# Chunk 4's first MLP layer by twenty block products, with chunk 5's substitution running on into chunk 4's second layer

## The chip, the cores and the metric

The kernel runs on one core of one Trainium2 chip. The time is that of the device in microseconds (us), from launch to end of one execution. TensorE is called PE, VectorE DVE, ScalarE ACT, GpSimd POOL, and SP is the engine whose queue issues nearly all DMAs. Instructions stand in a fixed order on each engine and the engines wait for each other by semaphores.

## The reference, cut to what matters

A DeltaNet layer (4 batches, 8 heads, 768 tokens, head size 48) is followed by an MLP of 3072 tokens, 384 inputs and 2048 hidden values, all in float32:

```python
for t in range(S):                      # per batch and head
    y[t]   = q[t] @ state
    v_old  = state.T @ k_n[t]           # k_n: k over its length
    state += beta[t] * outer(k_n[t], v[t] - v_old)
x = y.transpose(0, 2, 1, 3).reshape(B * S, H * D)
h = x @ w_in
g = h * (1.0 / (1.0 + np.exp(-h)))      # silu
out = g @ w_out
```

## The kernel before

The 768 tokens are cut into six chunks (0 to 5) of 128 tokens, each of two halves of 64. Within a chunk the recurrence is a triangular system; its 32 by 32 diagonal blocks are inverted and then merged to 64 by 64. For each chunk these stages run:

- `prepare`: scores of keys and queries, `ap`, and the blocks, which are laid out anew through DRAM to stand one system per partition (`blocks`, `g`).
- `invert` (L683 on): the substitution, on DVE alone. For m from 31 down to 1 two instructions each (L688 forms `rank`, L693 adds it to `x`), 62 in all, with 31 to 256 elements per partition. Then `g` (L706) and `x` (L697) are scaled. `g` is written to DRAM as `low` and read back as `xe` (L717), `x` as `up` and read back as `xi` and the rest of `xe`, all by SP's queue.
- `solve`: two merges on PE (`merge`, L847: the first reads `xe` and `ap` into `py`, which is copied to `y`; the second reads `xi`, `xe` and `y` into `px`, which is copied to `xi`), then for each half the keys on the state (`ph`, L893), the inner values (`pz`), the update of the state (`pu`, and L932 on DVE), and the outputs, which end as `xT`, the MLP's inputs, by ACT's copies and five DMAs.
- the MLP's first layer, silu on ACT, and the second layer `combine` (L1451), in seven chains of eight products for each half, with sums of the hidden values on DVE between (`sum_g`, L1428) and the output's parts added into `o` (L1462) by way of one tile `kept`.

Both layers save products by forming sums of blocks. The first layer of chunks 2 to 4 is `hidden_by_products` (22 items per half of the hidden blocks, 44 in all, each of two matmuls of 128 by 128 with 256 columns). Chunk 5 alone uses `hidden_by_chains` (`BY_CHAINS`): products of sums of weights and sums of inputs, in chains that add up in one PSUM bank, each partial result read out after its item. There are 40 items of two matmuls. Items go round four banks, so an item's bank was last written four items before, and must have been read out by then: the first result for an output is copied by ACT (16 items), the others are added by DVE (24 items, `evacuate`). The sums of weights (`W_SUMS`, 16 and two that restore a quarter of `w_in`) overwrite parts of `w_in`, so they can only be made once no later chunk needs the old form; the sums of inputs (`X_SUMS`) number twelve.

The order is written out by hand. The solve of chunk c+1 is laid between the second layer's products of chunk c, and the substitution of chunk c+1 between the first layer's items of chunk c. `run(n)` issues n pieces of the MLP; a piece of the second layer is half a chain, four products. `paced` issues the substitution: each item of the layer earns it a credit, less where DVE has an addition to make, and it steps as long as the credit is positive. `run_to(start(c) + ITEMS + 3)` sets how many pieces lie between the first layer's end and the solve. Every instruction is pinned behind the one before it on its engine, so what DVE makes late is late for all that stands behind it there.

## Time and profile before

| | us |
|---|---|
| median of three runs | 626.05 |
| single runs | 623.24, 626.05, 772.2 |
| the profiled execution | 622.51 |
| its span, first to last instruction | 620.8 |
| PE busy | 606.4 (98%) |
| DVE busy | 466.6 (75%) |
| ACT busy | 247.7 (40%) |
| chunk 3's second layer, with chunk 4's solve | 403.4 to 458.3 |
| chunk 4's first layer, with chunk 5's substitution | 458.3 to 496.3 |
| chunk 4's second layer, with chunk 5's solve | 496.3 to 545.7 |
| chunk 5's first layer | 545.7 to 580.6 |

The profile is one execution as the hardware recorded it; times in it are from the span's start. A row of the timeline has the start, the duration, the engine, the line, what is written and read, and how many instructions were run together; in brackets stands how long the engine had been idle and what it waited for. The table by stages gives for each stretch its length, and for each engine the busy time and the number of instructions.

### The profile page before, as it was taken

The page shows a single profiled execution, that of the slowest core. Times are in us where ns is not written, and L with a number is a line of the kernel's source. Part 1 is how long each engine was busy: PE and PEld are TensorE (multiplying, and loading weights), DVE is VectorE, ACT ScalarE, POOL GpSimd, SP SyncE. Part 2 cuts the span into 40 slices and gives each one's busy share as a digit, 9 for nine tenths or more (in the row PEclk, how much of TensorE's full clock was granted, in tenths as well). Part 3 has the DMA queues.
Part 4 walks back from the last instruction along what each step waited for, and adds up shares of the span by engine and source line. Part 5 has one row for each costly group of instructions (what it writes and reads, how often), then busy time and mean ns, then how long its engine had stood idle before and what let it go on. Part 6 is the DMA issues. An engine that isn't in the chain of part 4 may idle for free.

```text
span 620.8 us, 21912 instructions
## 1 busy us (share of the span) xinstructions
PE 606.4 (98%) x9554; PEld 531.2 (86%) x9554; DVE 466.6 (75%) x983; ACT 247.7 (40%) x562; POOL 82.7 (13%) x83
## 2 busy tenths in 40 slices
PE   8889999999999999999999999999999999999997
PEld 5678778666689988888899998899998899988997
DVE  5856879998889976768986769976869997535632
ACT  3656756142351133533433533434433414445310
POOL 5443621247000010000010000010000020000000
PEclk9859999999999999999999999999999999999999
DMA  7745654164426482236073436084351060110011
GB/s 156 181 101 167 219 141 106 52 162 117 114 48 132 93 145 51 66 80 123 0 150 92 103 78 122 1 157 105 87 111 34 1 112 17 40 25 1 2 25 26
DMA packets 143935, 55.06 MB, mean 89 GB/s; under 512 B 113488, under 2 KB 137296, under 8 KB 143840
## 3 DMA queue, kind: packets, MB, share of 16 engines
q1 hardware_dynamic: 143360, 53.00, 37.9%
q8 instruction: 75, 1.23, 0.8%
q10 hardware_dynamic: 480, 0.67, 0.3%
q14 instruction: 20, 0.16, 0.1%
HBM read 40.99 MB, written 10.49 MB: 83 GB/s over the span
## 4 chain that ended last, share of the span: by engine, by line
PE 56%; DVE 1%; issue 0%; ACT 0%; DVEq 0%; ACTq 0%
PE px L1451 14%; PE py L1451 10%; PE hu L1168 10%; PE hx L1168 8%; PE hx L1335 3%; PE hu L1335 3%; PE pa L585 2%; PE pz L905 1%; PE ph L893 1%; PE pyc L986 1%; PE pyc L973 1%; PE pu L925 1%; PE px L847 1%; PE py L847 1%; DVE kq L1285 1%
## 5 line engine op out<-in xcount | busy, mean ns | idle before, releaser
L1114 PE MATMUL phid<-xT,w_in 128*128 128x256 f32 x384 | 89.1, 385 | 0.2 <-issue 0.2
L1114 PEld LDWEIGHTS phid<-xT,w_in 128*128 128x128 f32 x384 | 71.0, 190 | 10.4 <-issue 0.8
L1451 PE MATMUL px<-sums_of_w,sums_of_g 128*128 128x192 f32 x320 | 58.0, 330 | 0.0
L1451 PE MATMUL py<-w_out,sums_of_g 128*128 128x192 f32 x320 | 57.5, 329 | 0.0
L1451 PEld LDWEIGHTS px<-sums_of_w,sums_of_g 128*128 128x128 f32 x320 | 52.1, 190 | 1.1 <-issue 0.7
L688 DVE SCALAR_TENSOR_TENSOR rank<-g,step,x 128x31 f32<-128x31 f32 (+15 forms) x124 | 49.6, 400 | 4.6 <-DMA g<-blocks 1.7
L1451 PEld LDWEIGHTS py<-w_out,sums_of_g 128*128 128x128 f32 x320 | 52.3, 190 | 0.6
L693 DVE TENSOR_TENSOR x<-x,rank 128x31 f32<-128x31 f32 (+15 forms) x124 | 42.5, 342 | 4.4
L521 POOL TENSOR_TENSOR vf<-vf,n_slot 128x768 f32<-128x768 f32 x10 | 15.4, 1552 | 189.9 <-DVE sums_of_g L1428 147.2
L1428 DVE TENSOR_TENSOR sums_of_g<-gT 128x512 f32<-128x512 f32 (+2 forms) x44 | 28.0, 668 | 13.3 <-PE py L1451 13.1
L1462 DVE TENSOR_TENSOR o<-o,kept 128x192 f32<-128x192 f32 (+1 forms) x29 | 12.4, 426 | 32.6 <-ACT kept L1459 32.4
L1168 PE MATMUL hx<-xT,w_in 128*128 128x256 f32 x144 | 36.0, 379 | 0.0
L600 ACT COPY gT<-hu 128x512 f32<-128x512 f32 x36 | 21.1, 586 | 32.9 <-PE hu L1168 22.9
L1168 PE MATMUL hu<-xT,w_in 128*128 128x256 f32 x144 | 34.0, 379 | 0.0
L600 ACT COPY xT<-pyc 48x128 f32<-48x128 f32 (+2 forms) x120 | 31.1, 260 | 1.6
L932 DVE TENSOR_TENSOR state<-state,pu 48x384 f32<-48x384 f32 x44 | 24.3, 552 | 8.8 <-PE pu L925 7.8
L1168 PEld LDWEIGHTS hu<-xT,w_in 128*128 128x128 f32 x144 | 27.4, 190 | 3.7
L1168 PEld LDWEIGHTS hx<-xT,w_in 128*128 128x128 f32 x144 | 27.3, 190 | 3.6
L1451 PE MATMUL px<-sums_of_w,gT 128*128 128x192 f32 x160 | 28.7, 329 | 0.2 <-issue 0.2
L1451 PE MATMUL py<-w_out,gT 128*128 128x192 f32 x160 | 28.9, 330 | 0.0
L1451 PE MATMUL px<-w_out,gT 128*128 128x192 f32 x160 | 28.5, 329 | 0.0
L1122 ACT ACTIVATE gT<-phid 128x512 f32<-128x512 f32 x24 | 14.4, 598 | 35.5 <-PE phid L1114 35.3
(264 smaller groups left out, 1243.4 us busy)
## 6 DMA issues: line engine op xcount, KB each, us to landing
vf<-in_v_dram SPq DMA_DIRECT2D x48, 96.0 KB, 2.7
out_dram<-o SPq DMA_DIRECT2D x42, 96.0 KB, 2.3
w_out<-in_moe_w_in_dram SPq DMA_DIRECT2D x12, 256.0 KB, 3.4
sums_of_w<-in_moe_w_out_dram SPq DMA_DIRECT2D x8, 384.0 KB, 3.6
blocks<-ap SPq DMA_DIRECT2D x40, 64.0 KB, 2.3
g<-blocks SPq DMA_DIRECT2D x4, 512.0 KB, 3.5
up<-x SPq DMA_DIRECT2D x4, 512.0 KB, 3.0
xi<-up SPq DMA_DIRECT2D x16, 128.0 KB, 3.5
```

The costliest lines, as they stand in the source:

```text
L521: done = pin(nc.gpsimd.tensor_tensor(out=vf, in0=vf, in1=of, op=ALU.mult))
L585: pin(nc.tensor.matmul(pa[e][half, p * n * W : (p + 1) * n * W], lhsT=kq[rows, p, 0, half], rhs=kq[rows, p, js[0] : js[-1] + 1, half], sta ...
L600: return pin(nc.scalar.copy(to, of))
L688: pin(nc.vector.scalar_tensor_tensor(out=tv, in0=g[:, 0:m, m : m + 1].to_broadcast([P, m, n]), scalar=step[:, m : m + 1], in1=x[:, m : m + ...
L693: yield pin(nc.vector.tensor_tensor(out=x[:, 0:m, m:T], in0=x[:, 0:m, m:T], in1=tv, op=ALU.add))
L932: pin(nc.vector.tensor_tensor(out=to, in0=to, in1=by_heads(pu[of]), op=ALU.add))
L1114: pin(nc.tensor.matmul(ph[:, j * GT : (j + 1) * GT], lhsT=w_in[:, a, (2 * f + j) * P : (2 * f + j + 1) * P], rhs=xTs[c, hf][:, a, :], star ...
L1122: pin(nc.scalar.activation(out=hidden_of(c, hf, f), in_=ph[:], func=ACTF.Silu, scale=0.5))
L1168: pin(nc.tensor.matmul(to[:, GT * i : GT * (i + 1)], lhsT=weights[:, f], rhs=moving, start=start and i == 0, stop=True, skip_group_check=True,
L1335: pin(nc.tensor.matmul(to[:, GT * i : GT * (i + 1)], lhsT=weights[:, 2 * u + i], rhs=moving, start=start and i == 0, stop=True, skip_group ...
L1428: pin(nc.vector.tensor_tensor(out=sums_of_g[:, k, fs], in0=of[0], in1=of[1], op=op))
L1451: pin(nc.tensor.matmul(to, lhsT=at, rhs=quarter(f, *b) if isinstance(b, tuple) else sums_of_w[b][:, f], start=start and n == 0, stop=n == ...
```

## The change

`BY_CHAINS` takes in chunk 4 (`NCH - 2`), so both last chunks form their first layer by 40 items. What follows from that:

- The 18 sums of weights are made one chunk earlier, in three blocks of six in chunk 3's second layer; they are ordered anew, since two of their rooms lie in the key buffer that chunk 4's solve still reads.
- The twelve sums of inputs are made for both chunks, in three parts (six ahead of the layer, four at its start, two after its ninth item), and in other rooms: `sums_of_g`, the key buffer and one part of `xT`. Before, they lay in `turned_kq`, which chunk 4 can't spare.
- In chunk 4's solve ACT makes all copies of `y` and `xi`, where it shared them with DVE.
- `paced` starts the substitution of chunk 5 at the first item (it was the fifth), with a credit of 0.84 for each item and 0.62 less behind an addition. The layer has 40 items, and seven pieces of the second layer (three before) stand between its end and the solve, which then takes two pieces fewer in its first steps.

DVE, at the seam of chunk 3's second layer and chunk 4's first. `ap` rows are the last masks, `o` rows the outputs of chunk 3, `gT<-gT,hx` an addition of the first layer, `rank` and `x` the substitution. Before:

```order
L595 TENSOR_TENSOR ap_6288<-pa_6311,above 128x4x64
L595 TENSOR_TENSOR ap_6288<-pa_6312,above 128x4x64
L1462 TENSOR_TENSOR o<-o,kept 128x192
L1462 TENSOR_TENSOR o<-o,kept 128x384
L1156 TENSOR_TENSOR sums_of_g<-xT 128x256
L1156 TENSOR_TENSOR sums_of_g<-xT,sums_of_g 128x256
L1156 TENSOR_TENSOR xT<-xT 128x256
L1156 TENSOR_TENSOR sums_of_g<-xT,sums_of_g 128x256
L1156 TENSOR_TENSOR sums_of_g<-xT 128x256
L1462 TENSOR_TENSOR o<-o,kept 128x192
L1183 TENSOR_TENSOR gT<-gT,hx 128x2x256
L688 SCALAR_TENSOR_TENSOR rank_6398<-g,step,x 128x31
```

The same place now, from the last two masks to the first substitution step:

```order
L595 TENSOR_TENSOR ap_6300<-pa_6323,above 128x4x64
L595 TENSOR_TENSOR ap_6300<-pa_6324,above 128x4x64
L1291 TENSOR_TENSOR w_in<-w_in 128x4x128
L1291 TENSOR_TENSOR sums_of_w_in<-w_in,sums_of_w_in 128x512
L1286 SCALAR_TENSOR_TENSOR kb_77<-w_in,sums_of_w_in 128x512
L1286 SCALAR_TENSOR_TENSOR kb_77<-kb_77,w_in 128x512
L1286 SCALAR_TENSOR_TENSOR w_in<-sums_of_w_in,w_in 128x4x128
L1291 TENSOR_TENSOR w_in<-w_in 128x4x128
L1471 TENSOR_TENSOR o<-o,kept 128x192
L1471 TENSOR_TENSOR o<-o,kept 128x384
L1291 TENSOR_TENSOR sums_of_g<-xT 128x256
L1291 TENSOR_TENSOR sums_of_g<-xT,sums_of_g 128x256 x2
```

Six sums of weights have come between the masks and the additions to `o`, and behind the rows shown follow three more input sums, the last `o` and four input sums before the first `rank`.

DVE, further into chunk 4's first layer, from the ninth step on (rows with 207 elements) to the first additions. Before, the first addition stood ahead of the first step, and the second behind the fourth; now:

```order
L688 SCALAR_TENSOR_TENSOR rank_6453<-g,step,x 128x207
L693 TENSOR_TENSOR x<-x,rank_6453 128x23x9
L1329 TENSOR_TENSOR gT<-gT,hx 128x2x256
L688 SCALAR_TENSOR_TENSOR rank_6459<-g,step,x 128x220
L693 TENSOR_TENSOR x<-x,rank_6459 128x22x10
L1329 TENSOR_TENSOR gT<-gT,hx 128x2x256
L1291 TENSOR_TENSOR xT<-xT,sums_of_g 128x256
L1291 TENSOR_TENSOR sums_of_g<-xT 128x256
L688 SCALAR_TENSOR_TENSOR rank_6470<-g,step,x 128x231
L693 TENSOR_TENSOR x<-x,rank_6470 128x21x11
```

Nine steps stand ahead of the first addition, which belongs to the seventh item (items 6 and 7, counted from 0, are the first that DVE adds). The last steps, and four sums of the second layer's inputs, stand behind all 24 additions.

PE, in chunk 4's second layer up to the first merge of chunk 5 (`py<-xe,ap`). Before and now:

```order
L1451 MATMUL px<-sums_of_w,gT 128x192 x8
L1451 MATMUL py<-w_out_110,sums_of_g 128x192 x2
L1451 MATMUL py<-w_out_109,sums_of_g 128x192 x2
L847 MATMUL py<-xe,ap_83 32x32 x64
L1451 MATMUL py<-w_out_109,sums_of_g 128x192 x2
```

```order
L1460 MATMUL px<-sums_of_w,gT 128x192 x8
L1460 MATMUL py<-w_out_109,sums_of_g 128x192 x4
L1460 MATMUL py<-w_out_110,sums_of_g 128x192 x4
L1460 MATMUL px<-sums_of_w,sums_of_g 128x192 x8
L1460 MATMUL py<-w_out_109,gT 128x192 x4
L847 MATMUL py<-xe,ap_83 32x32 x64
```

The merge stands behind nine half chains of the second layer, where it stood behind five.

The diff (lines of the new kernel are some nine further down, so L1183 and L1323 become L1329 for these items, L1285 L1291, L1428 L1437, L1451 L1460, L1462 L1471):

```diff
--- before.py
+++ after.py
@@ -850,10 +850,10 @@
         of = pm[:].rearrange("p (h t) -> p h t", h=HH)
         if second:
             for rows in (slice(0, T), slice(W, W + T)):
-                (by_act, by_dve)[g](xis[g][rows, :, T:W], of[rows])
+                (by_act, by_act if c == BY_CHAINS[0] else by_dve)[g](xis[g][rows, :, T:W], of[rows])
         else:
             for rows in (slice(T, W), slice(W + T, P)):
-                (by_act, by_dve)[g](y[rows, g], of[rows])
+                (by_act, by_act if c == BY_CHAINS[0] else by_dve)[g](y[rows, g], of[rows])
 
     def merge_half(g, hf, second):
 
@@ -1236,17 +1236,19 @@
                 CC.append(rooms[1])
             yield
 
-    BY_CHAINS = (NCH - 1,)
+    BY_CHAINS = (NCH - 2, NCH - 1)
     GROUPS = ((0, 1), (0, 0), (1, 1), (1, 0))
     W_SUMS = (
         (12, 4, 1, 3, -1), (3, 3, 1, 9, 1), (13, 4, -1, 3, 1), (14, 4, -1, 5, 1), (5, 5, 1, 8, -1), (4, 4, -1, 5, 1),
-        (15, 0, 1, 6, 1), (16, 4, -1, 15, -1), (17, 10, 1, 11, -1), (18, 2, -1, 17, -1), (19, 18, -1, 1, -1),
-        (15, 7, 1, 15, -1), (6, 6, -1, 7, 1), (1, 15, -1, 1, -1), (11, 13, 1, 11, -1), (11, 11, 1, 2, 1),
+        (15, 0, 1, 6, 1), (16, 4, -1, 15, -1), (17, 10, 1, 11, -1), (11, 13, 1, 11, -1), (11, 11, 1, 2, 1),
+        (15, 7, 1, 15, -1), (18, 2, -1, 17, -1), (19, 18, -1, 1, -1), (1, 15, -1, 1, -1), (6, 6, -1, 7, 1),
     )
     X_SUMS = (
-        (6, 2, 1, 4, 1), (7, 6, -1, 1, 1), (8, 1, -1, 0, -1), (9, 0, 1, 6, 1), (10, 1, 1, 3, 1), (11, 10, 1, 4, -1),
-        (12, 0, 1, 10, 1), (13, 12, 1, 2, 1), (14, 5, 1, 6, 1), (15, 5, 1, 4, 1), (16, 10, 1, 5, 1), (17, 14, 1, 3, 1),
+        ((6, 2, 1, 4, 1), (7, 6, -1, 1, 1), (14, 5, 1, 6, 1), (8, 1, -1, 0, -1), (15, 5, 1, 4, 1), (9, 0, 1, 6, 1)),
+        ((10, 1, 1, 3, 1), (11, 10, 1, 4, -1), (17, 14, 1, 3, 1), (16, 10, 1, 5, 1)),
+        ((12, 0, 1, 10, 1), (13, 12, 1, 2, 1)),
     )
+    X_ROOMS = {6: 0, 7: 1, 14: 2, 8: 3, 10: 4, 11: 5, 17: 6, 16: 7, 13: 1}
     CHAINS = (
         (
             ((12, 1, 3, -1), (13, 7, 7, 1), (9, 8, 6, -1), (3, 9, 2, 1)),
@@ -1270,10 +1272,14 @@
         return of[:, n * 4 * P : (n + 1) * 4 * P].rearrange("p (r t) -> p r t", r=4)
 
     def inputs_at(c, slot):
+        slot = 1 if slot == 12 else slot
         if slot < 2 * NKT:
             return xTs[c, slot % 2][:, slot // 2]
-        n = slot - 2 * NKT
-        return turned_kq[:].rearrange("p b j a t -> p (b j a t)")[:, n * GT : (n + 1) * GT]
+        if slot in X_ROOMS:
+            n, of = X_ROOMS[slot], sums_of_g[:].rearrange("p k f t -> p (k f t)")
+        else:
+            n, of = {15: 4, 9: 5}[slot], kbufs[NCH % 2][:].rearrange("p g r -> p (g r)")
+        return of[:, n * GT : (n + 1) * GT]
 
     def linear(to, a, of_a, b, of_b):
         if of_a < 0 and of_b < 0:
@@ -1292,8 +1298,8 @@
         for to, a, of_a, b, of_b in W_SUMS:
             yield linear(weights_at(to), weights_at(a), of_a, weights_at(b), of_b)
 
-    def sum_inputs(c):
-        for to, a, of_a, b, of_b in X_SUMS:
+    def sum_inputs(c, part=0):
+        for to, a, of_a, b, of_b in X_SUMS[part]:
             linear(inputs_at(c, to), inputs_at(c, a), of_a, inputs_at(c, b), of_b)
 
     def hidden_by_chains(c):
@@ -1329,6 +1335,7 @@
         orders = [[(n == 0, *one) for chain in side for n, one in enumerate(chain)] for side in CHAINS]
         items = [(side, u, *orders[side][n]) for n in range(len(orders[0])) for side in range(2) for u in range(2)]
         waiting, ready = None, deque()
+        sum_inputs(c, 1)
         for n, (side, u, start, w, x, o, sign) in enumerate(items):
             to, weights, moving = sides[side][u], weights_at(w), inputs_at(c, x)
             for i in range(2):
@@ -1343,6 +1350,8 @@
                     if not left[one[0:2]]:
                         ready.append((n + 2, *one[0:2]))
             waiting = (u, o, sign, to)
+            if n == 8:
+                sum_inputs(c, 2)
             while ready and (last or ready[0][0] <= n):
                 silu(*ready.popleft()[1:])
             if last:
@@ -1472,7 +1481,7 @@
                         sum_g(c, *(what if len(what) == 3 else (hf, *what)))
                 yield
 
-        first, then, sooner, ahead, parts = (), (), (), (), PARTS[::-1] if by_chains else PARTS
+        first, then, ahead, parts = (), (), (), PARTS[::-1] if by_chains else PARTS
         if c < 2:
             first, parts = ((S1, NG - 1), (S2, NG - 1)), range(NG)
         elif hf == 0:
@@ -1480,7 +1489,7 @@
         else:
             first = tuple((S2, fs) for fs in parts)
         if hf == 1 and c + 1 in BY_CHAINS:
-            sooner = (sum_inputs,)
+            ahead = (sum_inputs,)
         elif hf == 1 and c + 1 < NCH:
             ahead = (sum_x,)
         elif hf == 0 and c > 1:
@@ -1502,7 +1511,7 @@
         if last:
             store(c, hf, o, 0, left)
         yield
-        yield from steps(chain(px[:, left], 0, 0), *sooner)
+        yield from steps(chain(px[:, left], 0, 0))
         keep(px[:, left])
         add(o[:, 1].rearrange("p (n m) -> p n m", n=2), kept[:].unsqueeze(1).to_broadcast([P, 2, HM]))
         if last:
@@ -1895,11 +1904,15 @@
     go(long_2, 99)
     assert next(sums_made, 0) == 0
 
-    ITEMS, OUTPUT = 44, 14
+    OUTPUT = 14
+
+    def items_of(c):
+
+        return 40 if c in BY_CHAINS else 44
 
     def start(c):
 
-        return 2 * (NFF + OUTPUT) + (c - 2) * (ITEMS + 2 * OUTPUT)
+        return 2 * (NFF + OUTPUT) + sum(items_of(i) + 2 * OUTPUT for i in range(2, c))
 
     weight_sums = sum_weights()
 
@@ -1908,14 +1921,23 @@
         assert done[0] <= at
         run(at - done[0])
 
-    def paced(steps, first):
-
-        credit, m, left = 0.0, T - 1, True
-        for n in range(ITEMS):
+    def paced(c, steps, first):
+
+        credit, m, left, seen_by = 0.0, T - 1, True, set()
+        added = []
+        for n in range(5 * 2) if c in BY_CHAINS else ():
+            for side in CHAINS:
+                o = [one[2] for chain in side for one in chain][n]
+                added += [o in seen_by] * 2
+                seen_by.add(o)
+        for n in range(items_of(c)):
             run()
             if n < first:
                 continue
-            credit += 0.84 - (0.68 if n % 22 in (3, 6, 12, 14, 16, 18) else 0.0)
+            if added:
+                credit += 0.84 - (0.62 if n and added[n - 1] else 0.0)
+            else:
+                credit += 0.84 - (0.68 if n % 22 in (3, 6, 12, 14, 16, 18) else 0.0)
             while left and credit > 0.0:
                 left = next(steps, 0) != 0
                 credit -= 0.38 + 0.00225 * m * (T - m) if m > 0 else 1.2
@@ -1949,11 +1971,11 @@
 
     for c in range(2, NCH):
         solving, more = solve(c), c + 1 < NCH
-        if c in BY_CHAINS:
+        if c == BY_CHAINS[0]:
             go(weight_sums, 6)
         for n in range(8):
             go(solving)
-            run((1, 1, 2, 2, 1, 1, 2, 2)[n] if c == 2 else (2, 2, 2, 2, 1, 1, 2, 2)[n])
+            run((1, 1, 2, 2, 1, 1, 2, 2)[n] if c in (2, NCH - 1) else (2, 2, 2, 2, 1, 1, 2, 2)[n])
             if n == 2 and c > 2 and more:
                 assert done[0] >= start(c) - OUTPUT - 4
                 load_blocks(k, c + 1, G1)
@@ -1961,8 +1983,8 @@
                 load_blocks(q, c + 1, G0)
             if n > 0:
                 go(after, 8)
-            if c in BY_CHAINS:
-                go(weight_sums, {2: 4, 6: 8}.get(n, 0))
+            if c == BY_CHAINS[0] and n == 2:
+                go(weight_sums, 6)
         go(after, 99)
         go(solving)
         run()
@@ -1970,7 +1992,6 @@
         if c == 2:
             pieces = chained(pieces, *(feed_forward(c) for c in range(2, NCH)))
         if not more:
-            assert next(weight_sums, 0) == 0
             break
         run(1 if c == 2 else 2)
         step = block_steps(c + 1)
@@ -1982,10 +2003,11 @@
         go(sums_in)
         linked(load_v, c + 1)
         load_k(c + 2)
+        go(weight_sums, 99 if c == BY_CHAINS[0] else 0)
         run_to(start(c))
-        paced(invert(c + 1, step), 7 if c == 2 else 4)
+        paced(c, invert(c + 1, step), 7 if c == 2 else 0 if c in BY_CHAINS else 4)
         after = lengths(c + 2) if c + 2 < NCH else iter(())
-        run_to(start(c) + ITEMS + 3)
+        run_to(start(c) + items_of(c) + (7 if c in BY_CHAINS else 3))
         for g in range(2):
             size(c + 1, g)
         for n in range(4 if c == 2 else 2):
```

## The prediction

> **What bounds the kernel now.** I read the page's busy shares first, then the stages, then TensorE (PE) and VectorE (DVE) in order of time around chunk 4.
>
> ```profile
> PE 606.4 (98%) x9554; PEld 531.2 (86%) x9554; DVE 466.6 (75%) x983; ACT 247.7 (40%) x562; POOL 82.7 (13%) x83
> core 0: us, PE busy (x) PEld busy (x) DVE busy (x) ACT busy (x) POOL busy (x), PEclk, DMA share, GB/s
> 403.40:458.30 54.90, 54.90 (x1253) 51.98 (x1252) 41.09 (x85) 21.91 (x64) 4.02 (x4) 1.00 0.55 115
> 458.30:496.30 38.00, 38.00 (x178) 33.46 (x177) 32.66 (x79) 15.04 (x24) 0.00 (x0) 1.00 0.16 36
> 496.30:545.70 49.40, 49.40 (x1058) 47.13 (x1057) 37.75 (x63) 17.27 (x51) 3.68 (x2) 1.00 0.27 53
> ```
>
> PE never pauses in the three stages that the change touches: chunk 3's second layer (403.4 to 458.3), chunk 4's first layer (to 496.3) and chunk 4's second layer with chunk 5's solve inside (to 545.7). So a product taken away is worth its full time, and anything that makes PE wait costs in full. DVE has only 5.3 us free in chunk 4's first layer (38.00 less 32.66), and that is where the change puts more work.
>
> **What goes away.** PE's rows at the ends of the two first layers:
>
> ```profile
> 458.32 1.03 PE L1168 MATMUL hx<-xT,w_in 128*128 128x256 f32 x4
> ...
> 496.31 2.76 PE L1451 MATMUL px<-w_out,gT 128*128 128x192 f32 x16
> 498.91 2.76 PE L1451 MATMUL px<-sums_of_w,gT 128*128 128x192 f32 x16
> ...
> 502.90 1.29 PE L847 MATMUL py<-xe,ap 32*32 32x32 f32 x128
> ...
> 545.69 2.25 PE L1335 MATMUL hu<-xT,sums_of_w_in 128*128 128x256 f32 x8
> 547.78 1.89 PE L1335 MATMUL hx<-xT,w_in 128*128 128x256 f32 x8
> 549.50 1.89 PE L1335 MATMUL hu<-kq,sums_of_w_in 128*128 128x256 f32 x8
> 551.23 1.89 PE L1335 MATMUL hx<-kq,kb 128*128 128x256 f32 x8
> ```
>
> (A matmul leaves two records.) Chunk 4 now takes 37.99 us for 88 products of 256 columns, 0.432 each. The chained form has 40 items of two products: 80, so 34.54 us. **Gain 3.45 us.** Items of chunk 5 run at the same rate (547.78 to 551.23 is four items, 0.863 each).
>
> **What is added, first place: chunk 3's second layer.** The 18 sums of weights move there from chunk 4's. Their price, and what stands at the second block of six:
>
> ```profile
> 527.13 0.68 DVE L1285 TENSOR_TENSOR sums_of_w_in<-w_in 128x512 f32<-128x512 f32 x1
> ...
> 531.70 0.69 DVE L1285 TENSOR_TENSOR w_in<-w_in 128x512 f32<-128x512 f32 x1
> 419.53 1.18 ACT L600 COPY xi<-px 32x512 f32<-32x512 f32 x2 [2.17 <-PE px L847]
> 421.10 0.33 ACT L1459 ACTIVATE kept<-py 128x192 f32<-128x192 f32 x1 [0.39 <-PE py L1451]
> 421.46 0.36 DVE L1462 TENSOR_TENSOR o<-o,kept 128x192 f32<-128x192 f32 x1 [0.18 <-ACT kept L1459]
> 426.21 0.56 DVE L1462 TENSOR_TENSOR o<-o,kept 128x384 f32<-128x384 f32 x1 [3.29 <-ACT kept L1459]
> 428.99 2.30 DVE L932 TENSOR_TENSOR state<-state,pu 48x384 f32<-48x384 f32 x4
> 431.73 1.15 PE L893 MATMUL ph<-state,kq 48*64 48x48 f32 x64
> ```
>
> Eight such sums take 527.13 to 532.39, 0.66 each: a block of six is 3.9 us. The first block falls where DVE now waits or makes the copies that go to ACT, and costs nothing (uncovered, the 3.9 us would delay `vf`). The second is not quite covered. ACT now makes four copies of `xi` from 419.53 at 0.59, so `kept` comes 0.8 later, and `o` at 422.26 in place of 421.46. From there to the end of the small rows that follow are 1.46 us (421.46 to 422.92), then six sums: 427.6, so the next `o` is 1.4 late, and all behind it to `state` is back to back. `state` ends at 432.7 in place of 431.29, and the product `ph` that reads its last quarter stands at 431.73: **PE waits 1.0 us**. Bounds: 0, if the sums hide wholly in the 3.29 idle, to 2, if they run at 0.75. From here PE and DVE stand 1.0 later.
>
> **Second place: the seam.** The third block stands behind the last masks and before two additions to `o`:
>
> ```profile
> 451.37 1.62 DVE L595 TENSOR_TENSOR ap<-pa,above 128x256 f32<-128x256 f32 x4 [0.58 <-ACT ap L600]
> ...
> 456.29 0.56 DVE L1462 TENSOR_TENSOR o<-o,kept 128x384 f32<-128x384 f32 x1 [2.18 <-ACT kept L1459]
> ...
> 541.39 0.42 DVE L1285 TENSOR_TENSOR kq<-xT 128x256 f32<-128x256 f32 x1
> ...
> 545.78 0.55 DVE L1462 TENSOR_TENSOR o<-o,kept 128x384 f32<-128x384 f32 x1
> ```
>
> Masks end at 452.99, now 454.0; six sums to 457.9; the short `o` to 458.2. ACT's next `kept` must wait for that (one `kept` tile), so the long `o` comes at 458.8, 2.5 after the row above; input sums begin at 459.3. Twelve input sums took 541.39 to 545.78, 0.37 each; ten and one short `o` make 4.0 us. The first products stand at 459.3 (458.32 and 1.0) and need none of the sums until their fifth item, so PE starts in time, but **the substitution starts at 463.3, 4.0 us behind the layer**, and the pacing counts from the first item.
>
> **Third place: DVE's row in chunk 4's first layer.**
>
> ```profile
> 461.79 0.26 DVE L688 SCALAR_TENSOR_TENSOR rank<-g,step,x 128x31 f32<-128x31 f32 x1
> ...
> 480.18 0.69 DVE L1183 TENSOR_TENSOR gT<-gT,hx 128x512 f32<-128x512 f32 x1 [0.67 <-PE hx L1168]
> 480.78 0.47 DVE L688 SCALAR_TENSOR_TENSOR rank<-g,step,x 128x247 f32<-128x247 f32 x1
> ...
> 487.94 0.69 DVE L1183 TENSOR_TENSOR gT<-gT,hx 128x512 f32<-128x512 f32 x1 [0.25 <-PE hx L1168]
> ...
> 491.40 0.69 DVE L1183 TENSOR_TENSOR gT<-gT,hu 128x512 f32<-128x512 f32 x1 [0.24 <-PE hu L1168]
> ...
> 494.18 1.95 DVE L706 TENSOR_TENSOR g<-x,step 64x1024 f32<-64x1024 f32 x1
> 496.16 1.22 DVE L697 TENSOR_TENSOR x<-x,step 128x1024 f32<-128x1024 f32 x1
> 552.36 0.69 DVE L1323 TENSOR_TENSOR gT<-gT,hx 128x512 f32<-128x512 f32 x1 [5.22 <-PE hx L1335]
> ```
>
> Before, from the first step (461.79) to the last result (494.18) are 32.39 us with 1.16 idle: 31.23 of work for 62 instructions and 11 additions. Now 24 additions stand among the same 62: 13 more at 0.60 (480.18 to 480.78), 7.8; two input sums, 0.8; four sums of the second layer's inputs, 2.4. Together 42.2: `g` starts at 505.5 and ends at 507.4.
>
> Part of this PE feels at once. An addition starts 0.26 behind its item (552.36 against the item's end at 552.09), and the item four places on may not start before it is done. Item 6's addition now has nine steps ahead of it: adding the distances from row to row (0.54 for the first step to 0.88 for the ninth, from 461.79 on) gives 6.4, so it starts at 469.6 and ends at 470.3. Item 10 is due at 459.3 and 10 times 0.863, 467.9: PE waits 2.4 there, about 0.5 at item 11 and 0.5 at item 14, **3.4 in all**. Behind that DVE is level with PE again.
>
> **Fourth place: the way of `g` to the merge.** The merge (L847) reads `xe`, which `g` reaches by two transfers through DRAM:
>
> ```profile
> 496.16 0.45 SPq L104 DMA_DIRECT2D low<-g  x1
> 497.45 0.34 SPq L104 DMA_DIRECT2D up<-x  x1
> 499.12 0.97 SPq L717 DMA_DIRECT2D xe<-low  x2
> xe<-low SPq DMA_DIRECT2D x2, 128.0 KB, 2.5
> ```
>
> 2.96 us from the first issue to the second, 0.46 for the second of two, 2.5 to land: 5.9, with nothing queued ahead on SP. So the merge can start at 507.4 and 5.9, **513.3**. PE arrives at 459.3 + 34.5 + 3.4 + nine half chains of 1.30 (498.91 less 496.31 is two), 508.9, and waits 4.4. Bounds of the way: other transfers of these lines landed in 2.2 to 3.7, so 5.1 to 7.9.
>
> [...]
>
> **The sum.** In the old run 117.9 us lie from the merge's start (502.90) to the end (620.8); four half chains of 1.30 now stand before the merge, so 112.7 remain, less 0.4, since chunk 5's second item no longer waits for `kept` behind twelve sums (545.69 to 547.78 is 2.09 for two items of 0.863). 513.3 + 112.3 = 625.6 against 620.8: 4.8 more. By waits: 1.0 + 3.4 + 4.4 - 0.4 - 3.45 gives 4.95. The profiled execution was 622.51, 1.7 outside its span, so **627.4 us**. The median shown is 626.05 with single runs of 623.24 and 772.2; I go by the profiled one. Moving `y` and `xi` to ACT in solve(4) costs nothing beyond the 0.8 above; the other rooms for input sums cost nothing in bytes; the stores of `o` that SP now issues ahead of chunk 5's first `xT` moves are read much later, at the input sums.
>
> **Rivals.** *The pacing holds (10%).* The substitution hides in the products as the credits say; then 3.45 us are gained: **619.1**. It needs `g` some 8 us sooner than my row, so that the merge is ready by 504.5; for it speaks that the additions now stand in groups where DVE overlaps neighbours, against it the 4.0 us late start, which needs no overlap to be true.
>
> *DVE is only half as late (12%).* If the additions cost 0.47 in place of 0.60 (24 times 0.13), the state wait is hidden (1.0) and the way takes 5.1, the merge starts about 4.9 sooner, PE's waits just eat the gain: **622.5**. This is the point where it turns: a merge at 508.4.
>
> *The second merge waits too (10%).* It reads what comes back from `up`, issued behind `x`, 1.2 after `g`. Before, `x` was ready at 497.38 and the last return, issued at about 503, landed some 4 us later: 9.5 to 10.5 behind `x`; now 518.1 to 519.1. PE reaches it at 513.3 + 1.1 + 1.4 + 1.1 + 1.4 = 518.3, so 0 to 1 us; with landings at their slow end on both ways (3.7) it is 4 or more, **632 and above**.
>
> **How the numbers follow.** The forecast has 68%; its bounds, with DVE's row 1 shorter or 1.5 longer, are 624.6 (state 0, way 5.1) to 631.8 (state 2, way 7.9). Taking in the half-late case the range is 622 to 632, which leaves out the full gain and the slowest case. 2% is 12.5 us, about what a measurement of this kernel can tell from no change, and no case but the tail of the last reaches it: faster by over 2% 0.01, within 0.95, slower 0.04.
>
> **What would show it.** Right: PE idle for 2 to 3 us at the eleventh item of chunk 4's first layer, released by DVE's addition; `g` at L706 starting about 46 us behind that layer's first product; PE idle some 4 us before the first L847 of chunk 5, released by a DMA; a wait of about 1 us at L893 in chunk 3's second layer. Wrong: no idle at the first L847, or the substitution starting within 2 us of the first item. My sum fails if additions and substitution steps overlap more than the old rows show.

## The result, and the profile after

The changed kernel takes 632.34 us (median of four runs, 630.96 to 633.85), the kernel before 626.16 in the runs beside it: a ratio of 1.0115, 95% interval 1.0066 to 1.0163. The ratio is taken without the one slow run of 772.2. It is slower, by about 1%, inside the 2% that count as no change here. The profiled execution took 631.36, its span 629.6: 8.8 more than the 620.8 of before, where 4.8 more was forecast.

The page's busy shares after, and then the same three stages as before (chunk 3's second layer, chunk 4's first, chunk 4's second), in the columns of the table shown for before:

```profile
PE 608.0 (97%) x9538; PEld 531.8 (84%) x9538; DVE 471.9 (75%) x998; ACT 253.2 (40%) x574; POOL 82.9 (13%) x83
```

```profile
403.40:459.00 55.60, 55.17 (x1252) 52.04 (x1251) 47.88 (x94) 23.81 (x67) 4.02 (x4) 1.00 0.55 114
459.00:498.60 39.60, 36.72 (x162) 31.41 (x161) 36.87 (x85) 17.60 (x31) 0.00 (x0) 0.96 0.16 35
498.60:554.90 56.30, 52.43 (x1057) 49.49 (x1056) 29.86 (x56) 18.11 (x52) 3.73 (x2) 0.94 0.24 47
```

PE paused nowhere in these stages before. Now it is idle 0.43, 2.88 and 3.87 us, and in the column behind POOL stands something the prediction never looked at: the granted TensorE clock is 0.96 and 0.94 where it was 1.00. In chunk 4's first layer DVE is busy 36.87 of 39.60.

PE's waits for other engines in that part (what was waited for, us in all, how often, the longest):

```profile
PE py L847 <- DMA xe<-low: 3.6, 2, 3.1
PE hx L1342 <- DVE gT L1329: 2.9, 2, 2.6
PE ph L893 <- DVE state L932: 0.3, 1, 0.3
```

These are the three waits that were forecast, at their three places. PE's rows in time order around the first two, from chunk 4's first layer to the half chains behind the merge:

```profile
458.96 1.89 PE L1342 MATMUL hu<-xT,sums_of_w_in 128*128 128x256 f32 x8
...
470.39 1.13 PE L1342 MATMUL hx<-kb,sums_of_w_in 128*128 128x256 f32 x4 [2.64 <-DVE gT L1329]
471.77 2.05 PE L1342 MATMUL hx<-kb,sums_of_w_in 128*128 128x256 f32 x4 [0.25 <-DVE gT L1329]
473.62 2.70 PE L1342 MATMUL hu<-kb,w_in 128*128 128x256 f32 x8
476.15 1.89 PE L1342 MATMUL hx<-xT,kb 128*128 128x256 f32 x8
...
498.60 2.76 PE L1460 MATMUL px<-w_out,gT 128*128 128x192 f32 x16
...
513.55 0.32 PE L847 MATMUL py<-xe,ap 32*32 32x32 f32 x4 [3.10 <-DMA xe<-low]
514.34 1.91 PE L847 MATMUL py<-xe,ap 32*32 32x32 f32 x124 [0.47 <-DMA xe<-low]
516.19 2.93 PE L1460 MATMUL py<-w_out,gT 128*128 128x192 f32 x8
519.05 1.38 PE L893 MATMUL ph<-state,kq 48*64 48x48 f32 x64
520.36 1.57 PE L1460 MATMUL px<-sums_of_w,sums_of_g 128*128 128x192 f32 x8
```

Behind each wait the products themselves are slow. Items 10 to 13 take 5.76 (470.39 to 476.15), of which 0.25 is waiting; four items at full rate are 3.45, so 2.06 are lost. Behind the merge, one half chain takes 2.86 (516.19 to 519.05) where it took 1.40. From the merge's start to the half chain behind `ph` it is 6.81 now; the same three pieces took 3.69 before (502.90 to 504.12, 504.12 to 505.52, 506.92 to 507.99). Of the 3.12 more, 0.47 is waiting and 2.65 slow products.

The granted clock in stretches of 1 us around the two waits:

```profile
471.00:472.00 1.00, 0.75 (x4) 0.35 (x3) 1.00 (x3) 0.00 (x0) 0.00 (x0) 0.91 0.00 0
472.00:473.00 1.00, 1.00 (x3) 0.82 (x4) 0.93 (x4) 0.00 (x0) 0.00 (x0) 0.50 0.00 0
474.00:475.00 1.00, 1.00 (x4) 0.78 (x3) 1.00 (x3) 0.00 (x0) 0.00 (x0) 0.50 0.00 0
475.00:476.00 1.00, 1.00 (x6) 0.87 (x5) 0.97 (x3) 0.51 (x1) 0.00 (x0) 0.88 0.00 0
...
512.00:513.00 1.00, 0.00 (x0) 0.00 (x0) 1.00 (x1) 0.00 (x0) 1.00 (x2) 0.89 0.75 118
515.00:516.00 1.00, 1.00 (x90) 1.00 (x83) 0.00 (x0) 0.00 (x0) 0.00 (x0) 0.50 1.59 144
518.00:519.00 1.00, 1.00 (x4) 0.61 (x2) 0.00 (x0) 0.00 (x0) 0.00 (x0) 0.50 0.10 10
519.00:520.00 1.00, 1.00 (x49) 0.96 (x52) 0.36 (x1) 0.33 (x1) 0.00 (x0) 0.69 0.03 5
```

The clock falls to half, and stays there for a while with PE fully busy. In stretches of 0.1 us the column shows 1.00 up to 471.80, 0.62 in the next, and 0.50 from 471.90 to 475.20, so the clock is at either 1.0 or 0.5. A mean of 0.91 in a stretch of 1.00 then means 0.18 at half, so the first fall lasts from 471.82 to 475.24, 3.42 us; the second, by the same arithmetic, from 512.78 to 519.62, 6.84 us, twice as long.

DVE's row, from the end of `state` in chunk 3's second layer to `g`, and SP's row on the way of `g` to the merge:

```profile
430.03 2.29 DVE L932 TENSOR_TENSOR state<-state,pu 48x384 f32<-48x384 f32 x4
...
463.32 0.26 DVE L688 SCALAR_TENSOR_TENSOR rank<-g,step,x 128x31 f32<-128x31 f32 x1
...
469.65 0.68 DVE L1329 TENSOR_TENSOR gT<-gT,hx 128x512 f32<-128x512 f32 x1
...
506.26 1.97 DVE L706 TENSOR_TENSOR g<-x,step 64x1024 f32<-64x1024 f32 x1
```

```profile
508.26 0.45 SPq L104 DMA_DIRECT2D low<-g  x1
...
511.25 0.96 SPq L717 DMA_DIRECT2D xe<-low  x2
```

The substitution starts 4.36 behind the layer, `g` is done at 508.23, and the merge's matmuls come 5.3 (the first four) and 6.1 (the rest) behind that.

**A yardstick.** Execution times of one kernel spread by some 9 us here (622.3 to 631.3 for the kernel before), and much of that arises ahead of chunk 4: in the profiled runs below, the first product of chunk 4's first layer comes anywhere from 458.1 to 465.1. So I compare the time from that product to the end of the span as well. It is 162.5 before (620.8 less 458.32) and 170.6 after (629.6 less 458.96): 8.2 of the 8.8 lie there, 0.6 ahead of it. Each of these times is that of a single execution. Five of the runs below (after, later_merge, fill_merge, fill_merge_10, later_spread) are the same kernel up to the end of chunk 4's first layer, and take between 38.5 and 39.6 for that layer, so by this yardstick too a difference of 1 us between two runs says little.

### The profile page after: what moved, and what is told of

It reads as the page before. It is cut to its first block, busy times and chain, and to the rows that moved or that the text cites. A ratio compares the mean times of both kernels' runs of the same rounds, so it can differ in the third digit from the quotient of the medians.

```text
span 629.6 us, 21920 instructions
## 1 busy us (share of the span) xinstructions
PE 608.0 (97%) x9538; PEld 531.8 (84%) x9538; DVE 471.9 (75%) x998; ACT 253.2 (40%) x574; POOL 82.9 (13%) x83
## 5 line engine op out<-in xcount | busy, mean ns | idle before, releaser
L1460 PE MATMUL px<-sums_of_w,sums_of_g 128*128 128x192 f32 x320 | 58.1, 330 | 0.0
L1460 PE MATMUL py<-w_out,sums_of_g 128*128 128x192 f32 x320 | 57.2, 329 | 0.0
L1460 PEld LDWEIGHTS px<-sums_of_w,sums_of_g 128*128 128x128 f32 x320 | 52.1, 190 | 1.2 <-issue 0.7
L1460 PEld LDWEIGHTS py<-w_out,sums_of_g 128*128 128x128 f32 x320 | 52.3, 190 | 0.5
L600 ACT COPY gT<-hu 128x512 f32<-128x512 f32 x40 | 23.4, 585 | 40.7 <-PE hu L1342 25.4
L1437 DVE TENSOR_TENSOR sums_of_g<-gT 128x512 f32<-128x512 f32 (+2 forms) x44 | 28.0, 667 | 14.7 <-PE py L1460 14.6
L1471 DVE TENSOR_TENSOR o<-o,kept 128x192 f32<-128x192 f32 (+1 forms) x29 | 12.3, 425 | 32.3 <-ACT kept L1468 32.2
L1460 PE MATMUL py<-w_out,gT 128*128 128x192 f32 x160 | 30.3, 340 | 0.0
L1329 DVE TENSOR_TENSOR gT<-gT,hx 128x512 f32<-128x512 f32 x32 | 21.7, 685 | 11.4 <-PE hx L1342 11.2
L1460 PE MATMUL px<-sums_of_w,gT 128*128 128x192 f32 x160 | 28.7, 329 | 0.0
L1122 ACT ACTIVATE gT<-phid 128x512 f32<-128x512 f32 x24 | 14.4, 599 | 35.3 <-PE phid L1114 34.0
L1460 PE MATMUL px<-w_out,gT 128*128 128x192 f32 x160 | 28.5, 329 | 0.0
L905 PEld LDWEIGHTS pz<-vf,xi 64*64 64x64 f32 x768 | 25.3, 142 | 3.5 <-issue 3.1
L1460 PEld LDWEIGHTS py<-w_out,gT 128*128 128x128 f32 x160 | 27.2, 197 | 0.6 <-issue 0.3
L905 PE MATMUL pz<-vf,xi 64*64 64x48 f32 x768 | 27.3, 226 | 0.2 <-issue 0.2
```

The lines of the kernel that those rows point to most:

```text
L600: return pin(nc.scalar.copy(to, of))
L905: yield pin(nc.tensor.matmul(pz[rows, n * D : (n + 1) * D], lhsT=xis[g][rows, u * H + 2 * p + e, :], rhs=vfs[c][rows, hf, g * HB + u, p, : ...
L1122: pin(nc.scalar.activation(out=hidden_of(c, hf, f), in_=ph[:], func=ACTF.Silu, scale=0.5))
L1329: pin(nc.vector.tensor_tensor(out=to, in0=to, in1=of, op=ALU.add if same else ALU.subtract))
L1437: pin(nc.vector.tensor_tensor(out=sums_of_g[:, k, fs], in0=of[0], in1=of[1], op=op))
L1460: pin(nc.tensor.matmul(to, lhsT=at, rhs=quarter(f, *b) if isinstance(b, tuple) else sums_of_w[b][:, f], start=start and n == 0, stop=n == ...
```

## The experiments

My theory after the result: DVE's row (24 additions beside the substitution) and the way through DRAM set the merge's time, and what the prediction missed is that a pause of PE also costs clock. The rivals: PE's own waits are the loss and DVE would keep up without them; the slow products come from what runs beside them (the returns from DRAM, POOL), not from the pause.

| run | median, us | ratio to before, 95% interval | span | first product of chunk 4 to the end |
|---|---|---|---|---|
| before | 624.8 to 626.4 | | 620.8 | 162.5 |
| after | 632.34 | 1.0115 (1.0066 to 1.0163) | 629.6 | 170.6 |
| later_steps | 633.29 | 1.0110 (1.0044 to 1.0175) | 634.4 | 169.3 |
| later_merge | 630.55 | 1.0055 (1.0015 to 1.0095) | 627.6 | 166.5 |
| fill_merge | 636.18 | 1.0154 (1.0083 to 1.0224) | 631.2 | 170.9 |
| before_early | 632.08 | 1.0089 (1.0048 to 1.0130) | 626.2 | 167.5 |
| fill_merge_10 | 631.12 | 1.0119 (1.0066 to 1.0172) | 628.0 | 169.7 |
| early_w7 | 631.59 | 1.0085 (1.0046 to 1.0123) | 627.2 | 167.5 |
| before_early1 | 630.64 (one run) | | 628.9 | 164.8 |
| best7 | 628.04 | 1.0031 (1.0003 to 1.0060) | 626.6 | 164.9 |
| no_additions | 625.68 | 0.9999 (0.9974 to 1.0025) | 623.5 | 160.6 |
| later_spread | 627.56 | 1.0037 (1.0009 to 1.0065) | 622.8 | 164.7 |
| best_b | 624.90 | 0.9987 (0.9963 to 1.0012) | 622.4 | 162.2 |

**later_steps: is PE's wait in the first layer a loss of its own?**

```diff
-        paced(c, invert(c + 1, step), 7 if c == 2 else 0 if c in BY_CHAINS else 4)
+        paced(c, invert(c + 1, step), 7 if c == 2 else 4)
```

> The change, with chunk 5's substitution beginning behind the fifth item of chunk 4's first layer in place of the first. Theory one, DVE's row from the end of the input sums to g is the limit (its work is the same): the waits at items 10 and 11 (2.9) and the slower clock behind them (about 2.3) go, the layer ends near 494, but g still ends within 1 of 508.2, so PE's wait at the first merge grows from 3.6 to some 8, and the time stays at 632 (630 to 634). Theory two, PE's lateness in the first layer is a loss of its own: g comes with PE, the merge waits as before, and 5 us go: 627.

PE's wait for the addition in the first layer, its wait at the merge, and DVE's row of `g`, in the trace of this run (its layer starts at 465.07):

```profile
477.53 1.99 PE L1342 MATMUL hx<-xT,kb 128*128 128x256 f32 x8 [0.21 <-DVE gT L1329]
...
518.65 0.32 PE L847 MATMUL py<-xe,ap 32*32 32x32 f32 x4 [6.66 <-DMA xe<-low]
519.38 1.91 PE L847 MATMUL py<-xe,ap 32*32 32x32 f32 x124 [0.41 <-DMA xe<-low]
```

```profile
511.33 1.90 DVE L706 TENSOR_TENSOR g<-x,step 64x1024 f32<-64x1024 f32 x1
```

The wait of 2.89 in the layer shrinks to 0.21, and the layer runs in 35.0 in place of 39.6. The merge's wait grows from 3.57 to 7.07 and eats it: `g` starts 46.3 behind the layer's first product, after 47.3. Of 4.6 us taken from PE only 1.3 stay, and 1.0 of these is the `g` that comes sooner. DVE's row decides, as in theory one.

**no_additions: is DVE's row the whole loss?**

```diff
-                pin(nc.vector.tensor_tensor(out=to, in0=to, in1=of, op=ALU.add if same else ALU.subtract))
+                if c != BY_CHAINS[0]:
+                    pin(nc.vector.tensor_tensor(out=to, in0=to, in1=of, op=ALU.add if same else ALU.subtract))
```

> The change without its 24 additions on DVE in chunk 4's first layer (each output there keeps its first product alone, so the result is not the reference's); every product, sum of weights and step of the substitution stays. If DVE's row is the whole loss: no wait at items 10 and 11, L706 starts 14.4 (24 times 0.60) sooner, xe lands at some 41 behind the layer's first product while PE reaches the merge at 46, so no wait and no slow clock; from that product to the end 159.0 (162.5 of the kernel before less the 3.45 of eight products), plus up to 2 where PE runs through 128, 64 and 128 small matmuls with one half chain between them: 159 to 161, about 620. If something else of the change costs too (the other rooms of the input sums, the copies on ACT, the stage behind the merge): 163 or more.

From 462.89, its layer's first product, the rows of `g` and of the merge:

```profile
499.05 1.96 DVE L706 TENSOR_TENSOR g<-x,step 64x1024 f32<-64x1024 f32 x1
```

```profile
509.22 1.29 PE L847 MATMUL py<-xe,ap 32*32 32x32 f32 x128
```

The layer takes 34.54 (462.89 to 497.43), which is the 80 products at 0.432; the merge comes 46.3 behind the first product without a wait, and the clock is 1.00 behind it. 160.6 to the end, in the range expected. `g` came 11.1 sooner rather than 14.4, since DVE now waits in turn. So the 10 us between 170.6 and 160.6 all hang on DVE's additions; the new rooms and the stage behind the merge cost at most the 1.6 between 160.6 and 159.0, and 0.93 of that is one pause of PE at the second merge, of the kind shown below. The copies on ACT lie ahead of the layer, where this time doesn't reach; of them no run here shows a price of their own.

**fill_merge: does the pause lower the clock, or what runs beside it?**

```diff
+                for _ in range(20 if (c, hf, a, n) == (BY_CHAINS[0], 0, 0, 0) and start else 0):
+                    pin(nc.tensor.matmul(
+                        to, lhsT=at, rhs=quarter(f, *b), start=True, stop=True, skip_group_check=True,
+                    ))
```

> The change, with the first product of the third half-layer chain of chunk 4 repeated 20 times ahead of it (3.3 us of products whose result is overwritten, so the output is unchanged); PE comes to the first merge 3.3 later and has nothing to wait for but 0.3. No work is taken away. Theory one, the clock falls because of the idle time: behind the merge it stays at 1.00, merge and half chain take 1.2 and 1.4 in place of 2.64 and 2.86, and the time falls by about 3.2, to 629. Theory two, the slow stretch comes from what runs beside it: the clock falls to 0.5 as before and the time stays at 632.

The expectation has a slip: one such product takes 0.325 (eight in a chain of 2.60), so 20 are 6.5 us, 2.9 more than the wait they stand for. The trace answers the question all the same. The merge and the half chain behind it, and the 2 us ahead of the merge in the columns of the windows:

```profile
518.20 1.29 PE L847 MATMUL py<-xe,ap 32*32 32x32 f32 x128
519.41 1.57 PE L1464 MATMUL py<-w_out,gT 128*128 128x192 f32 x8
520.91 1.15 PE L893 MATMUL ph<-state,kq 48*64 48x48 f32 x64
```

```profile
516.00:518.00 2.00, 2.00 (x14) 1.97 (x13) 2.00 (x2) 0.33 (x1) 2.00 (x2) 1.00 1.34 150
```

With PE busy up to the merge, the clock stays at 1.00, while the DMA engines are as busy as after the change (1.34 against 1.19 to 1.59) and POOL works throughout. The merge takes 1.21 (518.20 to 519.41), the half chain 1.50. So theory two falls: the pause lowers the clock. (The first fall of the run after, at 471.82, came with POOL and DMA both at 0.00 in the columns shown above.) From the merge's start to the end it is 113.0 (631.2 less 518.20) against 116.05 after the change: the 0.47 of waiting and the slow products are gone there. In time nothing is won (170.9), because 2.9 us of the repeats come on top; 170.6 less 3.2 plus 2.9 is 170.3.

**fill_merge_10: the same with the right length.** The edit is `10` for `20`.

> As fill_merge, but 10 repeated products in place of 20: one takes 0.325, not 0.163 as I had it, so these are 3.25 us, which is the wait they stand for. From the first product of chunk 4's first layer to the end of the span it was 162.5 before, 170.6 with the change, 170.9 with 20 repeats. Theory one, idle time lowers the clock: PE comes to the merge with 0.3 to wait, the clock stays 1.00 over the merge and the half chain behind it, 3.2 us less: 167.4 from that product, about 629 in all. Theory two, what runs beside the merge slows it: 170.6 again, 632.

The clock is 1.00 over the merge and behind it, as said, but only 0.9 us are won, not 3.2. PE's waits in this run, "issue" being time in which it waited for nothing that the profile shows:

```profile
PE ph L893 <- issue: 1.9, 1, 1.9
PE px L847 <- issue: 0.9, 1, 0.9
```

In the middle of the 64 small matmuls of `ph`, PE stands still for 1.90, and at the second merge for 0.9: together 2.8 of the 3.2. Behind the merge at half clock these pauses were not there (after has no wait of 0.25 or more put down to "issue" at `ph` or at the second merge); some of what the slow clock cost would have been paid in another way. From the merge's start to the end it is 116.2 (628.0 less 511.83), so behind the merge nothing is won. later_merge and later_spread look at this.

The 0.9 that are won lie in the first layer. Its wait at item 10 is the same as after the change, and this time the clock stays at 1.00 behind it:

```profile
469.72 1.13 PE L1342 MATMUL hx<-kb,sums_of_w_in 128*128 128x256 f32 x4 [2.64 <-DVE gT L1329]
```

```profile
469.00:475.00 6.00, 4.75 (x20) 3.56 (x21) 5.83 (x14) 1.17 (x2) 0.00 (x0) 1.00 0.06 13
```

The layer takes 38.5 in place of 39.6, and `g` starts 46.2 behind its first product in place of 47.3. So a pause of this length doesn't lower the clock in every execution.

**before_early and before_early1: the price of a pause, with no work added.**

```diff
-        run_to(start(c) + ITEMS + 3)
+        run_to(start(c) + ITEMS + (0 if c == 4 else 3))
```

> The kernel before, with the first merge of chunk 5 three half chains earlier, at its end of chunk 4's first layer plus two: no work added or removed, but PE gets there at 499.0 while xe lands near 502.0 (g's end 496.1 and 5.9 of way). Theory one, idle time costs more than itself because the clock falls behind it: PE waits 3.0 at the merge and then runs at 0.5 to 0.8 for some 7 us, 3 us lost there; the wait itself is lost too, since the half chains that stood ahead of the merge come behind it: 6 in all, 632. Theory two, only the wait counts: 629. Theory three, the wait is hidden in later slack: 626.

The kernel before, with the merge three half chains sooner; PE's rows at the merge:

```profile
501.99 0.25 PE L847 MATMUL py<-xe,ap 32*32 32x32 f32 x4 [2.51 <-DMA xe<-low]
502.74 1.25 PE L847 MATMUL py<-xe,ap 32*32 32x32 f32 x124 [0.50 <-DMA xe<-low]
503.92 4.55 PE L1451 MATMUL px<-sums_of_w,gT 128*128 128x192 f32 x16
```

```profile
505.00:506.00 1.00, 1.00 (x5) 1.00 (x4) 0.99 (x2) 0.24 (x1) 0.00 (x0) 0.50 1.29 184
```

3.01 of waiting, then a chain of 4.48 (503.92 to 508.40) in place of 2.60 at a clock of 0.50: 1.9 us on top. The time to the end is 5.0 longer than before (167.5 against 162.5): 3.0, 1.9 and 0.1. That is theory one with a smaller second term than its 3, one fall of 3.42 us and not two.

> The kernel before, with the first merge of chunk 5 two half chains earlier in place of three (as in before_early). PE comes there at 500.3 and waits 1.2 to 1.8 in place of 3.0. Does so short a wait lower the clock? If a stretch of 3.4 us has to be mostly idle, no: products behind the merge at their usual 1.30 a half chain, and the time from chunk 4's first layer to the end is 1.2 to 1.8 more than the 162.5 of the kernel before. If any pause lowers it: 3.2 to 3.8 more.

Here it is `1` in place of `0`. The two waits and the stretch in which the slow chain of before_early would lie:

```profile
507.21 0.25 PE L847 MATMUL py<-xe,ap 32*32 32x32 f32 x4 [1.08 <-DMA xe<-low]
508.02 1.25 PE L847 MATMUL py<-xe,ap 32*32 32x32 f32 x124 [0.56 <-DMA xe<-low]
```

```profile
510.00:511.00 1.00, 1.00 (x8) 1.00 (x7) 0.97 (x2) 0.70 (x2) 0.00 (x0) 1.00 1.43 189
```

1.64 us of waiting leave the clock at 1.00, and the time to the end is 2.3 more than before: the wait, and 0.7 that I have not followed (one pause of 0.19 without a releaser is in it). So the price has a step: in these two runs the short pause cost itself and 0.7, the longer one itself and 1.9. A stretch of 3.42 at half clock costs at most half of itself, 1.7; the rest of the 1.9 is not explained.

**later_merge: a merge at which PE needn't wait.**

```diff
-        run_to(start(c) + items_of(c) + (7 if c in BY_CHAINS else 3))
+        run_to(start(c) + items_of(c) + (11 if c in BY_CHAINS else 3))
```

> The change, with the first merge of chunk 5 four half chains later (thirteen behind chunk 4's first layer in place of nine). Theory one, the granted clock falls because PE stood still for 3.6 us: no wait at the merge, clock 1.00 behind it, the merge takes 1.1 to 1.2 and the half chain behind it 1.4, so the wait's 3.6 and 3.2 of slow products go, 6.8 in all, less what chunk 5's inputs then come late (its last xT are issued 5.2 later against the old places, and now have 2.7 in hand: up to 3): 626 to 629. Theory two, the slow stretch is due to what runs beside the merge (the returns from DRAM, POOL's work), not to the idle time: the clock is 0.5 again behind the merge and only the wait's 3.6 go, less the same lateness: 629 to 632.

No wait for `xe`, clock 1.00 behind the merge, 4.1 us won to the end (166.5), within theory one's 6.8 less up to 3. (The median alone, 630.55, would have spoken for theory two; the clock column and the yardstick don't.) Behind chunk 5's first input sums DVE waits 1.18 for inputs (`xT`) that come late, and PE waits 0.25 for `kept`. What is missing stands in two rows, pauses that nothing releases:

```profile
521.69 0.91 PE L893 MATMUL ph<-state,kq 48*64 48x48 f32 x48 [1.29 <-issue]
...
525.81 0.21 PE L847 MATMUL px<-xe,y 32*32 32x32 f32 x1 [0.97 <-issue]
```

**later_spread: what these pauses hang on.** Behind chunk 5's first merge the change deals out the half chains one, one, two, two, where the kernel before had two, two, two, two: 128, 64 and 128 small matmuls then come with one half chain between them.

```diff
-            run((1, 1, 2, 2, 1, 1, 2, 2)[n] if c in (2, NCH - 1) else (2, 2, 2, 2, 1, 1, 2, 2)[n])
+            run((1, 1, 2, 2, 1, 1, 2, 2)[n] if c == 2 else (2, 2, 1, 1, 1, 1, 2, 2)[n] if c == NCH - 1 else (2, 2, 2, 2, 1, 1, 2, 2)[n])
```

> As later_merge, with the half chains behind chunk 5's first merge dealt out two, two, one, one in place of one, one, two, two. In later_merge PE stood still for 1.29 in the middle of the 64 small matmuls of L893 and for 0.97 at the second merge, and nothing the profile shows released it. If that comes of too many small matmuls in too short a time (128, 64 and 128 with one half chain between them), both pauses go: 164.2 from the layer's first product in place of 166.5. If the pauses have another cause, or the time only moves to the input sums of chunk 5: 166.5 again.

The pause at `ph` shrinks from 1.29 to 0.32 and the one at the second merge is gone; one of 0.48 stands at a later run of small matmuls. 164.7 to the end, 1.8 less, close to the 164.2 expected, but in part by luck: only 1.1 of it lie behind the merge (109.2 to the end in place of 110.3). The rest comes from the first layer, where the wait of 2.65 at item 10 did not lower the clock in this run (the layer takes 38.5, as in fill_merge_10) and 2.64 did in later_merge. The row at `ph`:

```profile
518.28 1.03 PE L893 MATMUL ph<-state,kq 48*64 48x48 f32 x56 [0.32 <-issue]
```

One pair of executions would not carry this, since the same order can give 0.5 (fill_merge) or 2.8 (fill_merge_10). Over all runs the order does tell: with two, two, two, two no such pause of 0.25 or more stands behind the merge (before, before_early, before_early1); with two, two, one, one they sum to 0.8 and 1.1 (later_spread, best_b); with one, one, two, two, where the clock is 1.00, to between 0.5 and 2.8 (five runs). So the pauses belong to the density of small matmuls, not to a fixed place. What PE waits for in them no trace shows.

**early_w7: DVE's row two microseconds shorter at the seam.** Three of the six sums of weights that stood at the seam move into an idle stretch of DVE in chunk 3's second layer (in `W_SUMS` the last sum goes ahead of the three that pass through slots 18, 19 and 1, so that the three to be moved come first).

```diff
-            if c == BY_CHAINS[0] and n == 2:
-                go(weight_sums, 6)
+            if c == BY_CHAINS[0]:
+                go(weight_sums, {2: 6, 7: 3}.get(n, 0))
```

> The change, with three of the third block's six sums of weights put a little earlier in chunk 3's second layer, ahead of the last four additions to the state, where DVE stands still for 1.3; the sums themselves are the same. Theory one, DVE's row decides: the substitution starts 2.0 sooner behind the layer's first product (2.4 in place of 4.4), item 10 waits about 0.7 in place of 2.6 and no slow clock follows, xe is ready 1.7 to 2.0 sooner, PE waits longer at the merge (some 6) because it comes sooner; from the layer's first product to the end 168.6 in place of 170.6. Up to 0.7 may come back as a wait for the state at L893. Theory two, PE's own waits in the first layer decide: 165.5 (both waits of item 10 and its slow stretch, 5.1, are gone).

167.5 to the end, 3.2 less, where theory one had 2.0 less. `g` starts 44.6 behind the layer's first product (504.33 less 459.74), 2.7 sooner; the waits in the first layer fall to 1.6 in three pieces of at most 1.1 and the clock does not fall there. At the merge PE waits 3.66 and the clock falls for two stretches as before. The substitution starts 1.6 sooner than after the change (2.8 behind the layer in place of 4.4); the other 1.1 of `g` is what the fall in the first layer cost (fill_merge_10, without moving a sum, has 46.2 for 47.3). So DVE's time comes back one for one, and the clock's share on top.

**best7 and best_b: put together.** Three of the sums earlier, the substitution behind the fifth item, the merge thirteen half chains behind the layer:

> Three parts together: the three sums of weights moved as in early_w7, the substitution begun behind the fifth item, and the first merge thirteen half chains behind the layer. If DVE's row and the way through DRAM set the merge: the layer runs in 34.8, PE comes to the merge at 34.8 and 16.9, 51.7 behind the layer's first product, xe is ready at 52.6 to 53.4, so 1 to 1.7 of wait, too short to lower the clock. Behind it 105 us remain (nine tenths of what the kernel before has there with nineteen half chains, less four of 1.30 and less 0.4, plus up to 1 for input sums that come late): 159 to 161 from the layer's first product, where the kernel before has 162.5: 622 to 625 in all, 1 to 3 below it. If the slow clock is not a matter of idle time, some 3 more: 164, 627.

164.9, 2.4 more than before: the range is missed. The layer ran in 34.5 as it should, but PE now came to the sixth chain ahead of its sums, which stand behind `g` and `x` on DVE:

```profile
511.48 4.29 PE L1460 MATMUL px<-sums_of_w,sums_of_g 128*128 128x192 f32 x16 [2.00 <-DVE sums_of_g L1437]
```

A wait of 2.00 and a chain of 4.08 (511.48 to 515.56) in place of 2.60: the step again. best_b starts the substitution behind the third item and deals the half chains as later_spread:

> Four parts together: three sums of weights moved as in early_w7, the substitution begun behind the third item, the first merge thirteen half chains behind the layer, the half chains behind it dealt out as in later_spread. If DVE's row and the way through DRAM are the only limits: the layer 35 (under 0.5 of wait), g done at 46.6 to 47.7 behind the layer's first product, about 1.1 of wait for the sums queued behind g, too short for the clock, the merge at 53.0 with xe there, and 107.1 behind it: 160 to 162, against 162.5 of the kernel before: 622 to 625. If a wait of 2 is left at those sums, as in best7, and the clock falls behind it: 164 to 165, and the kernel before is not beaten.

```profile
508.61 2.84 PE L1460 MATMUL px<-sums_of_w,sums_of_g 128*128 128x192 f32 x16 [0.19 <-DVE sums_of_g L1437]
...
512.68 1.47 PE L847 MATMUL py<-xe,ap 32*32 32x32 f32 x128
```

Waits of 0.19 are left, the clock is 1.00 from the first layer on, and the time to the end is 162.2 against 162.5: a ratio of 0.9987 (0.9963 to 1.0012). The change's loss is gone, but the kernel before is not beaten by anything this measurement can tell. The merge came at 52.5 behind the layer's first product, as worked out, but from there 109.7 pass (512.68 to 622.4) in place of 107.1: 1.1 of the difference are two pauses without a releaser (0.75 and 0.34), 0.25 a wait for `kept` in chunk 5's first layer; the rest I have not taken apart.

## Why the prediction was right or wrong

**Right in kind, short in size.** Slower was forecast, by three waits at three named places, and these are there. The span was to be 625.6 and is 629.6; the time was to be 622 to 632, with 627.4 as the forecast, and the median of 632.34 lies 0.3 above that range.

*What goes away:* 3.45 as said; no_additions shows the layer at 34.54.

*First place:* `state` ends 1.03 later than before (432.32 for 431.29) where 1.4 was worked out, and PE waits 0.3 at `ph`, not 1.0. The layer starts at 458.96, forecast 459.3.

*Second place:* the substitution starts 4.36 behind the layer; the sum said 4.0 and 463.3, and it is 463.32. That it fits to the hundredth is luck: the layer started 0.34 sooner and the row ahead of the substitution took 0.36 longer.

*Third place:* the first addition was put at 469.6 and starts at 469.65; PE's wait at items 10 and 11 was put at 2.4 and 0.5 and is 2.64 and 0.25. The 0.5 at item 14 did not come, because PE was itself slow by then: in fill_merge_10 and later_spread, where the clock stays at 1.00, PE waits 0.28 and 0.29 there. `L706` starts at 506.26 for 505.5.

*Fourth place:* the merge was put at 513.3 and starts at 513.55, with its other half at 514.34; the way took 5.3 and 6.1, worked out at 5.9. Here too two errors nearly cancel: `g` was done 0.8 later than worked out, and the first four matmuls came 0.6 sooner behind it. The last part of the wait, 3.57 in place of 4.4, is smaller because PE arrived at 510.45 and not 508.9.

**The step that failed is the sum:** "112.7 remain, less 0.4". From the merge's start to the end it is 116.05 (513.55 to 629.6), 3.75 more than the 112.3. Of these, 2.65 are slow products behind the wait and 0.47 the wait's second part; the remaining 0.6 stands in small pauses later. With the 0.25 by which the merge starts late, that is the whole gap of 4.0. The sum took it that PE, once released, runs at the rate it had before it paused. It priced each wait by its length alone. fill_merge, with the same order behind the merge and no pause ahead of it, has 113.0 there.

A price for the clock alone would not have made the term right, though. no_additions has the same order behind the merge too, no wait there and a clock of 1.00, and 114.3 remain (623.5 less 509.22), 2.0 above the 112.3: PE's pauses in the dense runs of small matmuls, 1.2 of it in two pauses, are a second part that the sum put at nothing.

The same mechanism worked in the first layer (2.06 us behind item 10, of which 0.5 are there at a clock of 1.00 as well: in fill_merge_10 the same four items take 3.99 without their wait, for 3.45). DVE's additions wait for PE's products, so it reached `g`: 47.3 behind the layer's first product with the fall (after, fill_merge), 46.2 without it (fill_merge_10, later_spread), which is what the prediction had (505.5 less 459.3). later_steps, which takes the wait and the fall away together, has 46.3: the fall cost DVE's row about 1.1, the wait itself almost nothing.

What the trace of before could have told: PE never paused in the three stages, so the clock stood at 1.00 in every row I quoted, and a column that never moves was not read as a term. But the column does move where PE pauses. The kernel's first 100 us before, in the same view:

```profile
0.00:100.00 100.00, 90.59 (x2419) 73.62 (x2420) 71.97 (x174) 56.60 (x125) 42.86 (x52) 0.91 0.63 162
```

PE is idle for 9.4 of these 100 us, and the clock is 0.91.

*The rivals.* "The pacing holds" fails by the additions, which are there in full; without them the time to the end is 160.6, where the rival's full gain would be 159.0. "DVE is only half as late" was wrong: the additions cost their 0.60. "The second merge waits too" did not happen: PE reached it at 521.86, 3.6 later than worked out, without a wait for `up`.

By waits: 0.64 ahead of the layer, 6.46 at the two places (2.64, 0.25, 3.10, 0.47), 4.71 of slow products (2.06, 2.65), less 3.45, is 8.4 of the 8.8.
